# Splitting an expert's first weight matrix into two 16-bit halves: stepping reads exchanged for stepping writes

## The chip, the cores and the metric

The kernel runs on one core of one Trainium2 chip. The metric is the time on the device in microseconds (us), the median of several executions. The engines are named as the profile names them: PE (matrix multiply), PEld (its weight load), DVE (vector engine), ACT (scalar engine), POOL (GpSimd) and SP (which issues transfers).

## The reference

The program is an attention over channels, whose output feeds a mixture of eight experts, each token going to one of them:

```python
qn = q / (norm(q, axis=1) + 1e-6);  kn = k / (norm(k, axis=1) + 1e-6)
a = softmax(kn.transpose(0, 2, 1) @ qn / tau)          # 256 x 256 for each of 4 batches
x = (v @ a).reshape(20224, 256)
e_idx = argmax(x @ w_gate, axis=1)                     # one of 8 experts for each token
for e in range(8):
    h = maximum(x[mask_e] @ w1[e], 0)                  # w1[e]: 256 x 1024
    out[mask_e] = gate_w * sigmoid(x @ w_output_gate)[e] * (h @ w2[e])   # w2[e]: 1024 x 256
```

The inputs are float32.

## The kernel before, in words

**Stages.** The grams (`gram`, L372) build k'q for four batches from streams of q and k; this takes the first part of the span together with `mix` (L528), which multiplies v by the attention matrix, picks an expert for each token (`route`) and scatters the rows by expert into memory. Then `blocks` (L1019) takes units of 256 tokens (the last ones of 128): it fetches rows and weights of an expert, forms h (`h_part`, L958), and from the unit before it y (`y_part`, L983), and scatters the result. The blocks of the first experts begin while `mix` still runs.

**Two halves for every number.** PE works on 16-bit floats for the experts. Each number is split into hi, its 16-bit rounding after a scale by a power of two, and lo, the 16-bit rounding of what is left. A product takes three matmuls (hi hi, hi lo, lo hi): L972 to L974 for h, L996 to L998 for y.

**The split of the weights** is `split` (L317), called once for w1 (`half` 0) and once for w2 (`half` 1) of each of the eight experts, 16 times in all. A tile `raw` of 128 partitions x 2048 float32 holds the matrix as it lies in memory. L328 takes the sum of squares in two passes of 1024 columns (written into hi as scratch), L333 and L334 add over the partitions, `root2` makes the scale `wsw`. Then the loop at L348 walks over cuts: for each, ACT writes hi (L349) and DVE writes lo = raw * scale - hi (L350), reading raw and hi.

For w2 there are two cuts of 1024 columns, read and written in order. For w1 there are four of 512 elements, and the order of the columns changes: a partition holds two rows of w1 of 1024 columns, `(c m f)` with c of 2, m of 128, f of 8, and h_part wants them as `(c f m)`, so that 128 neighbouring columns of a weight load have the same f. Neighbouring m are 8 float32 apart in `raw` (32 bytes); neighbouring f are 128 16-bit floats apart in hi and lo (256 bytes).

**Where the splits stand in the order of work.** Each engine runs its instructions in the order in which they were written. The split of expert 0 (`prep_first`) writes straight into the buffer that PE reads (`wbuf`) and stands within `mix` of the last batch. The splits of experts 1 to 7 (`prep`) go into `whi` and `wlo` (one buffer each, used by w1 and w2 in turn) and are stored to memory by `keep` (L358, issued by SP) for the blocks to fetch; they are spread over the steps of `blocks`. A step of `blocks` is one h_part and one y_part, 12 matmuls each for a full unit, with ACT's L976 (hi of h) and DVE's L977 (lo of h) behind the h_part. The generator yields after each second cut, so that a split of w1 puts two L349 on ACT and two L350 on DVE into one step and two more of each into the next, each pair behind the step's L976 and L977. PE reads h one unit later, from the tile `hb`; h's sums stand in PSUM in one of four buffers (`ps_x`) until L976 and L977 have read them.

Of the kernel before, what the change touches and what calls it, by code (L numbers as in the profile page):

```python
# [20 lines left out]
P = 128  # L21
# [17 lines left out]
def tile_colnorm_attention_then_top1_moe(  # L39
# [23 lines left out]
    CC = C // P  # L63
    FC = FF // P
# [154 lines left out]
    @contextmanager  # L219
    def behind(*engines):  # L220
        with ExitStack() as held_back:
            for e in engines:
                if e in last:
                    held_back.enter_context(tc.issue_after(last[e]))
            yield
# [10 lines left out]
    def pause(n):  # L236
        for _ in range(n):
            yield
# [17 lines left out]
    def root2(ss, kk, scale, inv):  # L256

        e = sm.tile(list(ss.shape), I32, tag="r2e", name="r2e")
        nc.vector.tensor_scalar(
            out=e, in0=ss.bitcast(I32), scalar1=24, scalar2=23,  # L260
            op0=ALU.logical_shift_right, op1=ALU.logical_shift_left,
        )
        nc.vector.tensor_scalar(
            out=scale.bitcast(I32), in0=e, scalar1=-1.0, scalar2=float((189 + kk) << 23), op0=ALU.mult, op1=ALU.add
        )
        nc.vector.tensor_scalar(
            out=inv.bitcast(I32), in0=e, scalar1=float((65 - kk) << 23), scalar2=None, op0=ALU.add
        )
# [19 lines left out]
    def prep(first, end, tag):  # L288
        todo = []
        for r in range(first, end):  # L290
            for half in range(2):
                with behind("SP"):
                    raw = load_raw(r, half, tag)
                todo.append(lambda raw=raw, half=half, r=r: in_turn(split(raw, half, r), "ACT", "DVE", "PE"))
                yield
                if len(todo) > AHEADW:
                    yield from todo.pop(0)()
        for f in todo:
            yield from f()

    def prep_first():

        raws = []
        for half in range(2):
            raws.append(load_raw(0, half, "raw"))
            yield
        yield from pause(RWAIT)
        parts = [in_turn(split(raw, half, 0), "ACT", "DVE", "PE") for half, raw in enumerate(raws)]
        for i in range(6):
            for part, since in zip(parts, (0, 2)):  # L310
                if i >= since:
                    next(part, None)
            yield
        for part in parts:
            yield from part

    def split(raw, half, r):  # L317

        rows = slice(r * P, (r + 1) * P)
        if r == 0:  # L320
            hi, lo = (wbuf[half][:, 0, n * HW1 : (n + 1) * HW1] for n in range(2))
        else:
            hi = big.tile([P, HW1], F16, tag="sp", name=f"whi{r}_{half}", bufs=1)
            lo = big.tile([P, HW1], F16, tag="sl", name=f"wlo{r}_{half}", bufs=1)
        ss = sm.tile([P, 2], F32, tag="wss", name="wss")
        for i in range(2):
            a = slice(i * HW1 // 2, (i + 1) * HW1 // 2)
            nc.scalar.activation(hi[:, a], raw[:, a], AF.Square, accum_out=ss[:, i : i + 1])  # L328
            yield
        yield from pause(WAITW)  # L330
        w_ps = ps_x.tile([P, 512], F32, tag="x", name="w_ps")
        tot = sm.tile([P, 1], BF16, tag="wtot", name="wtot")
        nc.vector.tensor_tensor(out=tot, in0=ss[:, 0:1], in1=ss[:, 1:2], op=ALU.add)  # L333
        nc.tensor.matmul(w_ps[:, 0:1], onesb, tot, start=True, stop=True)  # L334
        sw = sm.tile([P, 1], F32, tag="wsw", name="wsw")
        root2(w_ps[:, 0:1], KW, sw, invw[:, half, r : r + 1])

        if half == 0:
            src, dh, dl = (
                raw.rearrange("p (c m f) -> p c f m", c=CC, f=FC),  # L340
                hi.rearrange("p (c f m) -> p c f m", c=CC, f=FC),
                lo.rearrange("p (c f m) -> p c f m", c=CC, f=FC),
            )
            cuts = [(slice(None), c, slice(i, i + FC // 2)) for c in range(CC) for i in (0, FC // 2)]
        else:
            src, dh, dl = raw, hi, lo
            cuts = [(slice(None), slice(i * HW1 // 2, (i + 1) * HW1 // 2)) for i in range(2)]
        for i, a in enumerate(cuts):  # L348
            nc.scalar.activation(dh[a], src[a], AF.Copy, scale=sw)  # L349
            nc.vector.scalar_tensor_tensor(  # L350
                out=dl[a], in0=src[a], scalar=sw, in1=dh[a], op0=ALU.mult, op1=ALU.subtract
            )
            if i % 2:
                yield
        def keep():
            with behind("SP"):
                for n, part in enumerate((hi, lo)):
                    nc.sync.dma_start(wsc[half][rows, n * HW1 : (n + 1) * HW1], part)  # L358

        if r == 0:  # L360
            held.append(keep)
        else:
            keep()
        if half == 1:
            iw = invw[:, :, r : r + 1]
            nc.vector.tensor_tensor(out=iw[:, 0, :], in0=iw[:, 0, :], in1=iw[:, 1, :], op=ALU.mult)
            prepped.append(r)
# [763 lines left out]
```

## Time and profile before

| what | before |
|---|---|
| median of 3 runs | 1279.93 us (1278.78 to 1285.42) |
| the profiled execution, its span | 1285.2 us, span 1283.4 us |
| PE busy | 1201.1 us, 94% of the span |
| DVE, ACT, POOL busy | 702.2 us, 620.3 us, 572.5 us |
| L349 on 512 elements (w1), L350 on 512 elements (w1) | 32 each, 1217 and 1142 ns in experts 1 to 7 |
| L349 on 1024 elements (w2), L350 on 1024 elements (w2) | 16 each, 1141 and 1284 ns in experts 1 to 7 |

The profile was taken on one execution, 5.3 us above the median of the runs. "Busy" of PE counts its pipelined matmuls. A group's row gives the line, the engine, the operation, the tiles it writes and reads, the shapes, the count, its busy time and the mean time of one, and then how long the engine had been idle just before and what ended that. In the chain of waits each piece is followed back from the end of the program to what released it.

### The profile page before, as it was taken

The numbers are of one execution on the slowest core, as the hardware profiler recorded it, in microseconds if no ns is written. First come the engines' busy times: TensorE is split into PE (matmuls) and PEld (weight loads), VectorE is DVE, ScalarE is ACT, GpSimd is POOL, SyncE is SP. The second block draws the span as 40 slices with busy tenths as digits, with TensorE's granted clock in tenths as the row PEclk, the third lists the DMA queues.
The fourth block names the chain that finished last, engine by engine and source line by source line (L and its number), as shares of the span: only waits on it lengthen the run. The fifth ranks groups of instructions, "written<-read, shape, count | busy, mean of one in ns | idle before, by whom it ended". The sixth has DMA issues, their size and how long they took to land.

```text
span 1283.4 us, 27742 instructions
## 1 busy us (share of the span) xinstructions
PE 1201.1 (94%) x10412; PEld 1075.3 (84%) x10412; DVE 702.2 (55%) x2123; ACT 620.3 (48%) x1233; POOL 572.5 (45%) x561
## 2 busy tenths in 40 slices
PE   8999999997766989999999999999999899999998
PEld 7898888896755878888888888888888789999997
DVE  6666647544646765546464566544444454555552
ACT  5666557445633555545364556433333333444442
POOL 0004654555466123445454455544445454444443
PEclk9999999897989999999999999999999999999999
DMA  8976776754547895556555554843333534346743
GB/s 294 333 239 219 251 251 222 241 161 156 184 157 197 219 251 142 143 142 142 142 143 142 142 142 110 234 107 77 68 72 100 161 66 88 78 77 165 202 108 133
DMA packets 174594, 208.54 MB, mean 162 GB/s; under 512 B 120904, under 2 KB 123982, under 8 KB 169464
## 3 DMA queue, kind: packets, MB, share of 16 engines
q1 hardware_dynamic: 130312, 126.84, 35.7%
q0 software_dynamic: 43312, 79.73, 21.4%
q8 instruction: 84, 1.38, 0.4%
q14 instruction: 54, 0.44, 0.1%
q10 hardware_dynamic: 832, 0.16, 0.1%
HBM read 275.55 MB, written 61.41 MB: 263 GB/s over the span
## 4 chain that ended last, share of the span: by engine, by line
PE 75%; issue 8%; DMA 5%; DVE 4%; ACT 3%; POOL 2%; another core or an unknown queue 2%; POOLq 0%; SPq 0%; ACTq 0%; DVEq 0%
PE h_ps L974 9%; PE s_ps L409 9%; PE h_ps L972 9%; PE h_ps L973 9%; PE y_ps L998 9%; PE y_ps L996 9%; PE y_ps L997 9%; PE x_ps L549 3%; PE vt_ps L519 3%; PE x_ps L551 3%; PE x_ps L550 3%; DMA qk<-in_k_dram 2%; POOL out_dram L1009 1%; DMA wbuf<-wsc,wi 1%
## 5 line engine op out<-in xcount | busy, mean ns | idle before, releaser
L977 DVE SCALAR_TENSOR_TENSOR hb<-h_ps,hb 128x512 f16<-128x512 f32 (+1 forms) x360 | 227.1, 634 | 368.5 <-ACT hb L976 282.4
L972 PE MATMUL h_ps<-xt,wbuf 128*128 128x256 f16 (+1 forms) x1440 | 367.7, 263 | 8.5 <-issue 3.9
L974 PE MATMUL h_ps<-xt,wbuf 128*128 128x256 f16 (+1 forms) x1440 | 367.8, 263 | 3.6 <-issue 3.6
L973 PE MATMUL h_ps<-xt,wbuf 128*128 128x256 f16 (+1 forms) x1440 | 367.8, 263 | 3.5 <-issue 3.4
L996 PE MATMUL y_ps<-wbuf,hb 128*128 128x256 f16 x1296 | 354.4, 274 | 4.7 <-issue 3.4
L998 PE MATMUL y_ps<-wbuf,hb 128*128 128x256 f16 x1296 | 354.3, 274 | 3.6 <-issue 2.5
L997 PE MATMUL y_ps<-wbuf,hb 128*128 128x256 f16 x1296 | 354.4, 273 | 1.8 <-issue 1.6
L976 ACT ACTIVATE hb<-h_ps 128x512 f16<-128x512 f32 (+1 forms) x360 | 194.3, 550 | 328.8 <-PE h_ps L974 211.9
L627 POOL DMA_INDIRECT xs_d<-st,r_si x160 | 171.3, 1071 | 227.2 <-DVE r_si L623 91.5
L865 POOL DMA_INDIRECT wbuf<-wsc,wi x166 | 175.4, 1056 | 217.0 <-PE h_ps L974 154.0
L1009 POOL DMA_INDIRECT out_dram<-yo,b_id x162 | 168.9, 1043 | 76.0 <-issue 42.8
L972 PEld LDWEIGHTS <-wbuf 128*128 128x128 f16 x1440 | 141.6, 98 | 23.4 <-issue 5.5
L409 PE MATMUL s_ps<-qk 128*128 128x256 f32 x640 | 152.5, 389 | 8.8 <-DMA qk<-in_k_dram 6.3
L973 PEld LDWEIGHTS <-wbuf 128*128 128x128 f16 x1440 | 141.5, 98 | 21.0 <-issue 7.0
L974 PEld LDWEIGHTS <-wbuf 128*128 128x128 f16 x1440 | 141.6, 98 | 18.3 <-issue 4.6
L996 PEld LDWEIGHTS <-hb 128*128 128x128 f16 x1296 | 127.2, 98 | 21.7 <-issue 6.3
L998 PEld LDWEIGHTS <-hb 128*128 128x128 f16 x1296 | 127.2, 98 | 21.6 <-issue 4.6
L409 PEld LDWEIGHTS s_ps<-qk 128*128 128x128 f32 x640 | 120.8, 195 | 23.9 <-DMA qk<-in_q_dram 6.3
L997 PEld LDWEIGHTS <-hb 128*128 128x128 f16 x1296 | 127.2, 98 | 16.3 <-issue 2.1
L881 POOL DMA_INDIRECT xg<-xs_d,gi x49 | 50.8, 1037 | 178.5 <-DVE xr L947 157.7
L549 PE MATMUL x_ps<-ah,vh 128*128 128x272 f32 x320 | 104.5, 327 | 20.7 <-DVE rco L624 8.2
L397 DVE TENSOR_TENSOR acc<-acc,sq 128x1024 f32<-128x1024 f32 x76 | 92.8, 1222 | 44.9 <-ACT sq L396 29.1
(196 smaller groups left out, 1497.2 us busy)
## 6 DMA issues: line engine op xcount, KB each, us to landing
qk<-in_q_dram SPq DMA_DIRECT2D x76, 256.0 KB
qk<-in_k_dram SPq DMA_DIRECT2D x76, 256.0 KB
v<-in_v_dram SPq DMA_DIRECT2D x32, 512.0 KB
raw<-in_moe_w_dram SPq DMA_DIRECT2D x16, 1024.0 KB
xg<-xs_d SPq DMA_DIRECT2D x30, 272.0 KB
wsc<-whi SPq DMA_DIRECT2D x14, 512.0 KB
wsc<-wlo SPq DMA_DIRECT2D x14, 512.0 KB
v<-in_v_dram SPq DMA_DIRECT2D x8, 480.0 KB
```

The lines of the kernel that those rows point to most:

```text
L409: nc.tensor.matmul(s_ps[:, c, :], kt[:, 1, t, c * P : (c + 1) * P], qt[:, 0, t, :], start=st == 0 and t0 == 0 and t == 0 and c == 0 and n ...
L627: ins = nc.gpsimd.indirect_dma_start(out=xs_d[:, :], out_offset=bass.IndirectOffsetOnAxis(ap=si[:np_, t : t + 1], axis=0), in_=st[:np_, t, ...
L865: nc.gpsimd.indirect_dma_start(out=wbuf[half][:, at_of(u), :], out_offset=None, in_=wsc[half][:end, :], in_offset=bass.IndirectOffsetOnAxi ...
L972: nc.tensor.matmul(hp, w1s[:, 0, c, fs], xh, start=fi == 0 and c == 0, stop=False, **KWM)
L973: nc.tensor.matmul(hp, w1s[:, 0, c, fs], xl, start=False, stop=False, **KWM)
L974: main(PE=nc.tensor.matmul(hp, w1s[:, 1, c, fs], xh, start=False, stop=fin, **KWM))
L976: main(ACT=nc.scalar.activation(hh, h_ps[:, :, :w], AF.Relu))
L977: ins = nc.vector.scalar_tensor_tensor(out=hb[:, 1, 2 * fp : 2 * fp + 2, :w], in0=h_ps[:, :, :w], scalar=0.0, in1=hh, op0=ALU.max, op1=ALU ...
L996: nc.tensor.matmul(y_ps[:, t, :], hb[:, 0, f, tsl], w2s[:, 0, f, :], start=st, stop=False, **KWM)
L997: nc.tensor.matmul(y_ps[:, t, :], hb[:, 0, f, tsl], w2s[:, 1, f, :], start=False, stop=False, **KWM)
L998: main(PE=nc.tensor.matmul(y_ps[:, t, :], hb[:, 1, f, tsl], w2s[:, 0, f, :], start=False, stop=fin, **KWM))
L1009: ins = nc.gpsimd.indirect_dma_start(out=out[:, :], out_offset=bass.IndirectOffsetOnAxis(ap=un["id"][:, t : t + 1], axis=0), in_=un["yo"][ ...
```

## The change

In the four cuts of w1, ACT and DVE now go through `raw` in the order in which it lies in memory, and write hi and lo in steps. Before, they went through hi and lo in order and read `raw` in steps. The cuts are now halves of m (64 x 8 elements) where they were halves of f (4 x 128); each is still 512 elements, and the place of every number in hi and lo is as it was.

```diff
         if half == 0:
             src, dh, dl = (
-                raw.rearrange("p (c m f) -> p c f m", c=CC, f=FC),
-                hi.rearrange("p (c f m) -> p c f m", c=CC, f=FC),
-                lo.rearrange("p (c f m) -> p c f m", c=CC, f=FC),
-            )
-            cuts = [(slice(None), c, slice(i, i + FC // 2)) for c in range(CC) for i in (0, FC // 2)]
+                raw.rearrange("p (c m f) -> p c m f", c=CC, f=FC),
+                hi.rearrange("p (c f m) -> p c m f", c=CC, f=FC),
+                lo.rearrange("p (c f m) -> p c m f", c=CC, f=FC),
+            )
+            cuts = [(slice(None), c, slice(i, i + P // 2)) for c in range(CC) for i in (0, P // 2)]
```

The instructions stand where they stood, on every engine; only the shape of L349 and L350 for w1 is another. Here is DVE at the split of w1 of expert 1, with what each instruction waits for (`wlo` is lo, `whi` is hi, `raw` the float32 weights, `hb` the h of a block):

```order
-L350 SCALAR_TENSOR_TENSOR wlo_0_5184<-raw_0_5076,wsw,whi_0_5183 128x512 [waits DMAHW6_49,Activation_49]
-L350 SCALAR_TENSOR_TENSOR wlo_0_5184<-raw_0_5076,wsw,whi_0_5183 128x512 [waits Activation_49]
-L977 SCALAR_TENSOR_TENSOR hb<-h_ps,hb 128x512 [waits Activation_49]
-L350 SCALAR_TENSOR_TENSOR wlo_0_5184<-raw_0_5076,wsw,whi_0_5183 128x512 [waits Activation_49] x2
+L350 SCALAR_TENSOR_TENSOR wlo_0_5184<-raw_0_5076,wsw,whi_0_5183 128x64x8 [waits DMAHW6_49,Activation_49]
+L350 SCALAR_TENSOR_TENSOR wlo_0_5184<-raw_0_5076,wsw,whi_0_5183 128x64x8 [waits Activation_49]
+L977 SCALAR_TENSOR_TENSOR hb<-h_ps,hb 128x512 [waits Activation_49]
+L350 SCALAR_TENSOR_TENSOR wlo_0_5184<-raw_0_5076,wsw,whi_0_5183 128x64x8 [waits Activation_49] x2
```

Nothing moved, and each L350 waits for the same engines as before. On ACT, at the same place (`whi` is written by L349):

```order
-L349 ACTIVATE whi_0_5183<-raw_0_5076,wsw 128x512 [waits DVE_49,Activation_49]
-L349 ACTIVATE whi_0_5183<-raw_0_5076,wsw 128x512
-L976 ACTIVATE hb<-h_ps 128x512 [waits PE_49]
-L349 ACTIVATE whi_0_5183<-raw_0_5076,wsw 128x512 [waits Activation_49]
-L349 ACTIVATE whi_0_5183<-raw_0_5076,wsw 128x512
+L349 ACTIVATE whi_0_5183<-raw_0_5076,wsw 128x64x8 [waits DVE_49,Activation_49]
+L349 ACTIVATE whi_0_5183<-raw_0_5076,wsw 128x64x8
+L976 ACTIVATE hb<-h_ps 128x512 [waits PE_49]
+L349 ACTIVATE whi_0_5183<-raw_0_5076,wsw 128x64x8 [waits Activation_49]
+L349 ACTIVATE whi_0_5183<-raw_0_5076,wsw 128x64x8
```

Here too the order and the engines waited for are the same: although the two cuts of one c now interleave in hi, the second L349 does not wait for DVE.

## The prediction, made before the changed kernel ran

> **What bounds the kernel now.** I read first the shares of the engines and the chain of waits, then the stretches in which splits run, then the rows of the two changed lines.
>
> ```profile
> PE 1201.1 (94%) x10412; PEld 1075.3 (84%) x10412; DVE 702.2 (55%) x2123; ACT 620.3 (48%) x1233; POOL 572.5 (45%) x561
> PE 75%; issue 8%; DMA 5%; DVE 4%; ACT 3%; POOL 2%; another core or an unknown queue 2%; POOLq 0%; SPq 0%; ACTq 0%; DVEq 0%
> ```
>
> PE is the bound, with 82 us of the span not busy. ACT and DVE are half idle; a change in them counts only where PE runs dry behind them. Where the splits run, the windows say (columns: stretch, length, busy time and count of PE, PEld, DVE, ACT, POOL, granted clock, transfers):
>
> ```profile
> 345.00:356.00 11.00, 8.85 (x66) 8.47 (x65) 9.70 (x26) 11.00 (x21) 9.15 (x7) 0.84 0.22 78
> 420.00:440.00 20.00, 19.80 (x183) 17.50 (x181) 15.44 (x57) 12.76 (x22) 4.47 (x5) 1.00 0.86 218
> 600.00:660.00 60.00, 59.23 (x540) 52.32 (x538) 33.62 (x93) 32.24 (x59) 30.70 (x29) 1.00 0.54 139
> 700.00:835.00 135.00, 15.92 (x14) 1.00 0.58 155
> L349 ACT ACTIVATE wbuf<-raw,wsw x6: 1187/1226/1302, 345.7 to 353.5; 128x512 f16<-128x512 f32 x4, 128x1024 f16<-128x1024 f32 x2
> L349 ACT ACTIVATE whi<-raw,wsw x42: 1132/1212/1232, 430.3 to 828.6; 128x512 f16<-128x512 f32 x28, 128x1024 f16<-128x1024 f32 x14
> ```
>
> (The fourth row counts L349 alone on ACT.) Two regimes. From 345 to 356 us, where expert 0 is split inside the last batch's mixing, ACT is busy for 11.00 of 11 us and PE for 8.85: **ACT bounds this stretch.** From 430 to 829 us, experts 1 to 7 are split and PE is full: 59.23 of 60 us, 0.110 us for each of 540 matmuls. Here the splits cost only what PE waits for behind them:
>
> ```profile
> PE w_ps L334 <- DVE wtot L333: 5.8, 6, 4.0
> PE y_ps L998 <- DVE hb L977: 1.2, 3, 0.6
> PE y_ps L998 <- DVE hb L977: 0.2, 1, 0.2
> PE y_ps L998 <- DVE hb L977: 0.6, 1, 0.6
> ```
>
> The first two rows are PE's waits from 320 to 860 us (total, times, longest), the last two those at the w1 splits of 430 and 738 us. So of seven w1 splits two just reach PE, by 0.2 and 0.6 us; five stay below it. The wait for `wtot` is for the squares ahead of the changed lines.
>
> **The change, part by part.** Nothing is added, moved or taken away: 4 of L349 and 4 of L350 for each of eight experts, 32 and 32, change their access patterns. Their price before, beside the same lines and their neighbours in order:
>
> ```profile
> L349 ACT ACTIVATE whi<-raw,wsw 128x512 f16<-128x512 f32 x28 | 32.7, 1217 | 7.3 <-DVE invw L266 7.3
> L349 ACT ACTIVATE whi<-raw,wsw 128x1024 f16<-128x1024 f32 x14 | 15.3, 1141 | 15.7 <-DVE invw L266 15.5
> L946 ACT ACTIVATE xr<-xg,b_sx 128x256 f16<-128x256 f32 x162 | 74.2, 500 | 81.3 <-DVE b_sx L249 76.8 <-DVE wtot L333 2.1 <-DVE p2e L248 1.7
> L350 DVE SCALAR_TENSOR_TENSOR wlo<-raw,wsw,whi 128x512 f16<-128x512 f32 x28 | 31.3, 1142 | 9.7 <-ACT whi L349 9.7
> L350 DVE SCALAR_TENSOR_TENSOR wlo<-raw,wsw,whi 128x1024 f16<-128x1024 f32 x14 | 17.4, 1284 | 8.5 <-ACT whi L349 7.3 <-issue 1.2
> L947 DVE SCALAR_TENSOR_TENSOR xr<-xg,b_sx,xr 128x256 f16<-128x256 f32 x162 | 71.9, 479 | 3.5 <-ACT xr L946 1.9 <-issue 0.8 <-ACT whi L328 0.7
> ```
>
> L946 and L947 do on 256 elements in order what L349 and L350 do. ACT in order: (1141 - 500) / 768 = 0.835 ns an element, so 500 + 256 x 0.835 = 714 ns for 512; with the 32-byte steps it takes 1217, **503 ns more** (0.98 an element). DVE in order: (1284 - 479) / 768 = 1.048 ns, so 747 ns for 512; it takes 1142, **395 ns more** (0.77 an element).
>
> *What ACT saves and pays.* The stepping read goes, a stepping write comes: one stream in order, one not, as before. No row shows a long stepping write; the nearest are short:
>
> ```profile
> L605 ACT CAST st<-ids 128x8 int32<-128x8 f32 x20 | 4.2, 212 | 3.4 <-DVE acc L421 1.9 <-DVE r_d L584 0.7 <-issue 0.6
> L601 ACT ACTIVATE r_og<-r_og 128x8 f32<-128x8 f32 x20 | 4.3, 214 | 10.2 <-DVE r_og L600 6.1 <-DVE r_os L598 3.7 <-issue 0.4
> ```
>
> L605 writes 8 words at steps of a row of `st` (272 words), L601 8 in order: no difference, where a price like the read's would be 8 ns, about their scatter; tens of ns an element are excluded. Ends: 714 ns (stepping writes are free) and 1720 (they cost twice what the reads did, 1217 + 503, since each is half a word). I take 1217, the read's price, because the nearest row of size is the same line with one stepping stream.
>
> *What DVE saves and pays.* Reading `raw` in steps goes. But L350 also reads hi, which now lies in steps for it, and it writes lo in steps: **one stepping stream becomes two.** The price of the second input can be read:
>
> ```profile
> L728 DVE SCALAR_TENSOR_TENSOR tb_sl<-jf,tb_res 128x62 f32<-128x62 f32 x1 | 0.2, 216 | 0.0
> L731 DVE SCALAR_TENSOR_TENSOR tb_sl<-tb_sl,tb_g 128x62 f32<-128x62 f32 x1 | 0.3, 265 | 0.0
> L738 DVE SCALAR_TENSOR_TENSOR tb_ex<-tb_res,tb_g 128x62 f32<-128x62 f32 x1 | 0.3, 257 | 0.0
> L490 DVE SCALAR_TENSOR_TENSOR al<-s_sb,se,ah 128x256 fp32r<-128x256 f32 x8 | 3.6, 482 | 0.7 <-ACT ah L489 0.7
> ```
>
> All three of the first are the same operation on 62 elements; L731 and L738 read the second input at steps of 9 words (36 bytes). They take 41 to 49 ns more, 0.66 to 0.79 an element, which is what L350 pays on its first input. (L490 reads at steps of 8 bytes and pays nothing against L947's 479: the step's size matters.) So the stepping read of hi alone brings 747 + 340 = 1087 to 747 + 405 = 1152 ns: DVE has nothing to win, even where its writes are free. Ends: 1087, and 1547 where the write adds another 395. I take 1200: the two streams step at the same elements, so I let them mostly overlap.
>
> The Trainium skill bears on this choice in "Vector Engine (DVE) Microarchitecture Reference", section "Measured stream behaviour on trn2": with one source hopping every element it has 1.73 ns an element, with the output hopping 1.71, with all three 1.98, and it says that read and write penalties only partly add. The before row agrees with the first, (1142 - 211) / 512 = 1.82 with 211 ns of fixed time. By its 1.98 an estimate for L350 is 211 + 512 x 1.98 = 1225 ns; by its row of 2.5 for the output stepping 24 words, 1491.
>
> *The sum.* In the first stretch ACT changes by 4 x 0 and DVE by 4 x (1.200 - 1.158) = 0.2 us, behind ACT's 11.00 of 11 us: 0 to 0.2 us. In the PE stretch look at two steps around 431 us, ACT's rows first:
>
> ```profile
> 430.31 2.33 ACT L349 ACTIVATE whi<-raw,wsw 128x512 f16<-128x512 f32 x2
> 432.55 0.58 ACT L976 ACTIVATE hb<-h_ps 128x512 f16<-128x512 f32 x1
> 433.03 2.33 ACT L349 ACTIVATE whi<-raw,wsw 128x512 f16<-128x512 f32 x2
> 431.56 2.25 DVE L350 SCALAR_TENSOR_TENSOR wlo<-raw,wsw,whi 128x512 f16<-128x512 f32 x2 [1.54 <-ACT whi L349]
> 433.73 0.68 DVE L977 SCALAR_TENSOR_TENSOR hb<-h_ps,hb 128x512 f16<-128x512 f32 x1
> 434.33 2.21 DVE L350 SCALAR_TENSOR_TENSOR wlo<-raw,wsw,whi 128x512 f16<-128x512 f32 x2
> L350 DVE SCALAR_TENSOR_TENSOR wbuf<-raw,wsw,wbuf 128x512 f16<-128x512 f32 x4 | 4.6, 1158 | 0.7 <-ACT wbuf L349 0.7
> ```
>
> A pair and its L976 take ACT 2.72 us, a pair and its L977 take DVE 2.77, against 24 x 0.110 = 2.63 us of PE for a step. They fall behind by 0.1 us a step, and PE lives on what was done before. Behind the pair stand L977 and the L913 to L947 of the next unit, and for L977 waits PE. Four L350 of 58 ns more make DVE 0.23 us later at each split; at the two splits without reserve PE waits 0.23 us longer each, 0.5 us. Sum: 0 + 0.2 + 0.5, **0.7 us at most, on 1285.2 us of the profiled execution**. That execution lay 5.3 us above the median; I put the sum on the median, 1279.93 + 0.6 = **1280.5 us**. If the cover were gone everywhere, the same 58 ns would cost 28 x 0.058 = 1.6 us.
>
> **The rivals.** *Stepping writes are free on ACT.* [...] ACT saves 4 x 0.503 = 2.0 us in its own stretch. In the PE stretch DVE's first L350 starts 0.5 us earlier, which can take away no more than the 0.2 + 0.6 us that PE waits: 2.8 us, 1277.1 us. The waits for `wtot` are the only other reserve near, 5.8 us; earlier splits might win part of it. Were all of it won, 8.6 us, 1271.3.
>
> *Stepping 16-bit writes cost more than the reads did: slower.* Place: DVE's L977 behind the L350 pairs, and PE's y behind it. Each half word goes to another place than the last, and L350 has it beside a stepping read. At the upper ends, L350 takes 405 ns more and L349 503. A split then comes 4 x 0.405 = 1.6 us later by DVE, 4 x 0.503 = 2.0 by ACT. With DVE alone: the two splits without reserve cost 3.2 us, the five others between 0 and 1.6 each, 4.0 in the middle, the first stretch 0.5: about 8 us. With ACT too: 2.0 in the first stretch, 4.0, and 5.0 from the five: 11 us, 1291. I put the rival at 1289. It decides from about 6.4 us on, when L350 reaches some 1.45 us. Against it: L605, and that each write goes to a port other than the read's.
>
> *The two interleaved cuts bring a wait that was not there* (the second L349 for DVE's first L350, about 1.1 us a pair). Against it stands the order of both engines, in which the waits are on the same engines. 2 in 100. *That the change does nothing at all*, because both patterns are run in one order, is excluded by the new shape of 64 x 8.
>
> The Trainium skill has a rule, "SBUF — State Buffer", under the 16-byte cachelines of section "Door 1: The DMA port swizzle", that an access to a new line each time is penalised, whichever way. L490's free 8-byte steps and L731's paid 36-byte ones agree for reads. By it both patterns pay, and it gives my forecast for ACT.
>
> **How the numbers follow.** A difference below 0.5%, 6.4 us, is about what a measurement of this kernel can tell from none: its three runs span 6.6 us. Forecast (nothing seen, within 3 us): 0.55, which gives 0.52 same, 0.02 slower, 0.01 faster. ACT's writes free: 0.23; of this 0.15 stays within 0.5%, 0.08 goes beyond. Slower rival: 0.20, of which 0.16 beyond 0.5% and 0.04 within. New wait: 0.02, slower. Sums: faster 0.09, same 0.71, slower 0.20. The range for 8 in 10 reaches from below the free writes, 1274, to about the slower rival, 1290.
>
> **What will show it.** L349 on 512 elements near 1217 ns (1100 to 1350) and L350 near 1200 (1090 to 1300) bear the two prices out; 714 on ACT is the first rival, 1450 or more on DVE the second. ACT should still fill its stretch near 345 us, with its four L349 at about 1.26 us; PE's waits for L977 at the w1 splits should stay below 2 us in total. The forecast is wrong if L350 is above 1450 ns and the total still within 3 us (then PE had more reserve than I give it), or if the prices hold and the time moves by more than 6 us (then something else than these two lines moved).

## The result and the profile after

| | kernel before | changed kernel |
|---|---|---|
| median, us (lowest to highest, runs) | 1282.06 (1278.78 to 1285.42, 4) | 1326.05 (1318.88 to 1332.19, 4) |
| profiled execution, us | 1285.2 | 1332.19 |
| its span, us | 1283.4 | 1330.5 |

The changed kernel is slower: the ratio is 1.0341 with a 95% interval of 1.0264 to 1.0418, 44 us by the medians. (Here and below, runs over 1.5% slower than the fastest of their kernel are left out of the ratios, so that a ratio is not always the quotient of the two medians.) The forecast was 1280.5 us, "nothing seen", with a range up to 1290 us. It was wrong.

Shares of the engines and the chain of waits, changed kernel:

```profile
PE 1223.3 (92%) x10412; PEld 1085.7 (82%) x10412; DVE 742.9 (56%) x2123; ACT 658.5 (49%) x1233; POOL 573.8 (43%) x561
PE 52%; issue 6%; DVE 5%; DMA 4%; ACT 2%; POOL 2%; another core or an unknown queue 1%; POOLq 0%; DVEq 0%; ACTq 0%; SPq 0%
```

The counts of instructions are those of before. ACT has 38 us more to do and DVE 41. PE is still the engine with the least idle time, and the chain, which ran through PE for 75% before, now does so for 52%.

The rows of the changed lines, changed kernel (form and count, then busy us and mean ns of one, then the idle time before):

```profile
L349 ACT ACTIVATE whi<-raw,wsw 128x512 f16<-128x512 f32 x28 | 67.9, 2673 | 6.8 <-DVE invw L266 6.4 <-issue 0.4
L350 DVE SCALAR_TENSOR_TENSOR wlo<-raw,wsw,whi 128x512 f16<-128x512 f32 x28 | 67.0, 2542 | 18.8 <-ACT whi L349 13.2 <-issue 5.5
L349 ACT ACTIVATE wbuf<-raw,wsw 128x512 f16<-128x512 f32 x4 | 9.8, 2716 | 0.0
L350 DVE SCALAR_TENSOR_TENSOR wlo<-raw,wsw,whi 128x1024 f16<-128x1024 f32 x14 | 17.4, 1281 | 8.7 <-ACT whi L349 6.2 <-issue 2.4
```

Here is the surprise. A stepping L349 takes 2673 ns, where reading in steps took 1217; L350 takes 2542 where it took 1142. The forecast had 1217 and 1200, and its upper ends were 1720 and 1547. The split of w2, which steps nowhere, is unchanged in the last row (1284 before). So each w1 split has 4 x 1.456 = 5.8 us more on ACT and 4 x 1.400 = 5.6 us more on DVE.

**Where the 47.1 us between the two spans lie.** I measured from the start of one w1 split (its first L349) to the start of the next. The windows below (columns: stretch, length, busy time and count of PE, PEld, DVE, ACT, POOL, granted clock, transfers) cover five such stretches together, the second to the sixth. Before:

```profile
471.80:795.10 323.30, 318.49 (x2890) 281.58 (x2888) 186.09 (x525) 170.99 (x310) 151.59 (x145) 1.00 0.56 140
```

Changed, the same work:

```profile
480.10:831.60 351.50, 329.37 (x2887) 284.90 (x2886) 210.81 (x525) 194.19 (x311) 155.15 (x145) 0.97 0.51 129
```

The work is the same (2890 and 2887 matmuls), but the five stretches together are 351.5 - 323.3 = 28.2 us longer, 5.6 us a split. Of this PE is idle for 22.1 us where it was for 4.8, so 17.3 us are waiting. The other 10.9 us are PE "busy" longer for the same matmuls at a granted clock of 0.97 where it was 1.00. The remaining 18.9 us of the difference are spread: 4.0 us ahead of the first of these seven splits (expert 0's stretch in the main), 4.3 and 6.5 us in the stretches after the first and the seventh split, 4.1 us in the long rest, where w1 is no longer split. Not all of these are waits for h: in the stretch after the seventh split PE waits 3.7 us for weights from memory, and in the rest one such wait is 6.3 us where it was 2.5.

The main waits of PE in those five stretches (total, times, longest), before and then changed:

```profile
PE w_ps L334 <- DVE wtot L333: 1.3, 4, 0.8
PE y_ps L998 <- DVE hb L977: 0.6, 1, 0.6
```

```profile
PE y_ps L998 <- DVE hb L977: 11.6, 8, 2.3
PE y_ps L996 <- DMA wbuf<-wsc,wi: 1.8, 1, 1.8
PE y_ps L996 <- ACT hb L976: 1.8, 2, 1.6
```

It is the wait that the slower rival named: PE's y matmuls behind L977 on DVE, and L977 behind the L350 pairs. L977 and L976 together account for 12.8 of the 17.3 us. The chain of waits through one split (start, duration, what) shows both parts of the loss:

```profile
548.21 2.58 ACT whi L349
...
550.81 4.79 DVE wlo L350 x2
555.61 0.53 DVE hb L977
...
556.18 0.28 PE y_ps L998
556.46 0.11 PE y_ps L996
...
556.99 0.21 PE h_ps L974
557.20 0.21 PE h_ps L972
...
559.98 0.21 PE y_ps L997
560.19 0.12 PE y_ps L998
560.31 0.11 PE y_ps L996
```

One L349 and two L350 keep L977 waiting from 548.21 to 555.61, 7.4 us, where before the same stretch of the chain ran from 430.31 to 433.73, 3.4 us. PE had stopped for 2.25 us when it came to L998 at 556.18. Then, from 556.8 to 560.1 us, matmuls follow each other every 0.21 us instead of every 0.11: about 16 matmuls at twice the time, some 1.6 us more.

That second part was no term of the forecast. In the timeline of PE the five stretches hold six such runs of 16 slow matmuls. Four of them follow a wait for L977, one a wait of 1.85 us for weights and one a stop of 2.12 us that the profile calls issue. In the two splits whose longest wait is 1.2 us (those at 618.6 and 689.3) none follows for some 10 us. The length of a stop alone does not decide it, though: a stop of 2.24 us at 442.23 was followed by matmuls at the full rate. The Trainium skill, "TensorE: Matmul & The Clock Gate", in "What's actually happening", describes a clock that falls to half after an idle window of about 3.4 us and rises again after as much busy time. The halved rate and the 3.4 us of its length agree with this trace; its length of the idle time does not, since here a stop of 2.25 us was enough. What decides it is left open.

### The profile page after: what moved, and what is told of

Its sections match the earlier page's. It is cut to its first block, busy times and chain, and to the rows that moved or that the text cites. A ratio compares the mean times of both kernels' runs of the same rounds, so it can differ in the third digit from the quotient of the medians.

```text
span 1330.5 us, 27742 instructions
## 1 busy us (share of the span) xinstructions
PE 1223.3 (92%) x10412; PEld 1085.7 (82%) x10412; DVE 742.9 (56%) x2123; ACT 658.5 (49%) x1233; POOL 573.8 (43%) x561
## 4 chain that ended last, share of the span: by engine, by line
PE 52%; issue 6%; DVE 5%; DMA 4%; ACT 2%; POOL 2%; another core or an unknown queue 1%; POOLq 0%; DVEq 0%; ACTq 0%; SPq 0%
PE y_ps L998 9%; PE y_ps L996 9%; PE y_ps L997 9%; PE h_ps L974 9%; PE h_ps L973 9%; PE h_ps L972 8%; DMA wbuf<-wsc,wi 3%; DVE wlo L350 2%; ACT whi L349 1%; DMA wsc<-whi 1%; POOL out_dram L1009 1%; DVE hb L977 1%; POOL wbuf L865 1%; ACT hb L976 0%
## 5 line engine op out<-in xcount | busy, mean ns | idle before, releaser
L977 DVE SCALAR_TENSOR_TENSOR hb<-h_ps,hb 128x512 f16<-128x512 f32 (+1 forms) x360 | 229.6, 642 | 366.9 <-ACT hb L976 290.5
L972 PE MATMUL h_ps<-xt,wbuf 128*128 128x256 f16 (+1 forms) x1440 | 371.7, 266 | 17.7 <-DMA wbuf<-wsc,wi 9.3
L974 PE MATMUL h_ps<-xt,wbuf 128*128 128x256 f16 (+1 forms) x1440 | 372.5, 266 | 3.7 <-issue 3.6
L973 PE MATMUL h_ps<-xt,wbuf 128*128 128x256 f16 (+1 forms) x1440 | 372.3, 266 | 3.6 <-issue 3.3
L998 PE MATMUL y_ps<-wbuf,hb 128*128 128x256 f16 x1296 | 357.5, 276 | 17.1 <-DVE hb L977 16.0
L976 ACT ACTIVATE hb<-h_ps 128x512 f16<-128x512 f32 (+1 forms) x360 | 198.5, 562 | 329.5 <-PE h_ps L974 251.1
L865 POOL DMA_INDIRECT wbuf<-wsc,wi x166 | 173.9, 1048 | 228.1 <-PE h_ps L974 155.2
L972 PEld LDWEIGHTS <-wbuf 128*128 128x128 f16 x1440 | 142.9, 99 | 32.5 <-DMA wbuf<-wsc,wi 10.5
L409 PE MATMUL s_ps<-qk 128*128 128x256 f32 x640 | 155.2, 394 | 9.5 <-DMA qk<-in_k_dram 6.3
L973 PEld LDWEIGHTS <-wbuf 128*128 128x128 f16 x1440 | 143.0, 99 | 23.8 <-issue 8.6
L974 PEld LDWEIGHTS <-wbuf 128*128 128x128 f16 x1440 | 143.1, 99 | 21.6 <-issue 6.6
L998 PEld LDWEIGHTS <-hb 128*128 128x128 f16 x1296 | 128.3, 99 | 36.1 <-DVE hb L977 19.1
```

The source lines that it names most:

```text
L409: nc.tensor.matmul(s_ps[:, c, :], kt[:, 1, t, c * P : (c + 1) * P], qt[:, 0, t, :], start=st == 0 and t0 == 0 and t == 0 and c == 0 and n ...
L865: nc.gpsimd.indirect_dma_start(out=wbuf[half][:, at_of(u), :], out_offset=None, in_=wsc[half][:end, :], in_offset=bass.IndirectOffsetOnAxi ...
L972: nc.tensor.matmul(hp, w1s[:, 0, c, fs], xh, start=fi == 0 and c == 0, stop=False, **KWM)
L973: nc.tensor.matmul(hp, w1s[:, 0, c, fs], xl, start=False, stop=False, **KWM)
L974: main(PE=nc.tensor.matmul(hp, w1s[:, 1, c, fs], xh, start=False, stop=fin, **KWM))
L976: main(ACT=nc.scalar.activation(hh, h_ps[:, :, :w], AF.Relu))
```

## The experiments

Each run is compared with the kernel before on its own chip, since chips differ by more than the effect. Before took 1286.03 us beside the two one-engine runs and the spread run; 1220.69 beside the control of the spread run, the first doubled run, expert 0 alone and the first version without steps; and 1299.62 beside the others.

Two questions were open. Is the price one of the written pattern, or of two engines that write into the same region at the same time? And does the time come from that price where DVE and ACT stand before PE, or from something else that the change moved?

### The price of each pattern by itself

512 elements, six times each, engines apart, and at the end both at once. The patterns that decide (`hop(t, s)` has neighbours s elements apart and returns to the next column after eight; `walk(t, s)` moves on by s and never returns; `runs` and `rung` write r neighbours before each hop):

```python
nc.scalar.activation(**act(mf(H), mf(raw)))               # L67  all in order
nc.scalar.activation(**act(in4(H), step8(raw)))           # L69  read in steps (before)
nc.scalar.activation(**act(hop(H, 128), mf(raw)))         # L71  write in steps (changed)
nc.scalar.activation(**act(walk(H, 16), mf(raw)))         # L77  one half word in each 32 bytes
nc.scalar.activation(**act(walk(H, 2), mf(raw)))          # L79  one half word in each 4 bytes
nc.scalar.activation(**act(runs(H, 2), runs_src(raw, 2))) # L81  pairs of half words, 256 bytes apart
nc.scalar.activation(**act(hop(F, 64), mf(raw)))          # L85  32-bit words, 256 bytes apart
nc.vector.scalar_tensor_tensor(**dve(mf(L), mf(raw), mf(H)))              # L95  all in order
nc.vector.scalar_tensor_tensor(**dve(hop(L, 128), mf(raw), hop(H, 128)))  # L99  changed
nc.vector.scalar_tensor_tensor(**dve(mf(L), mf(raw), hop(H, 128)))        # L101 only hi read in steps
nc.vector.scalar_tensor_tensor(**dve(hop(L, 128), mf(raw), mf(H)))        # L103 only lo written in steps
nc.vector.scalar_tensor_tensor(**dve(rung(L, 2), mr(raw, 2), mr(H, 2)))   # L111 pairs of half words, 32 bytes apart
nc.vector.scalar_tensor_tensor(**dve(hop(G, 64), mf(raw), mf(H)))         # L115 32-bit words, 256 bytes apart
```

> Leaves out the whole computation: on 512 elements in 128 partitions, ACT's scaled copy and DVE's raw * scale - hi run six times each in a number of access patterns, first ACT, then DVE, and at the end both at once in the changed pattern. In the changed kernel L349 took 2673 ns and L350 2542, which is 4.66 and 4.55 ns an element on the fixed times. Theory W (a stepping 16-bit write has its own price on each engine): ACT alone in the changed pattern 2.6 to 2.7 us; DVE with only the output stepping 2.5, with only hi read in steps 1.1, with both 2.5; both engines at once no more than alone. Theory C (the price comes of both engines stepping at once): each alone 1.2 to 1.3 us, and 2.6 at once. What the price hangs on, if W: if half words (a write of part of a word), then 32-bit writes in the same steps cost 1.2 us or less, a half word alone in its word at any step 2.6, and runs of two half words 1.2; if the step of 256 bytes, then steps of 264 bytes cost 1.2 and 32-bit writes at 256 bytes 2.6; if coming back to the neighbouring half word soon after, then a walk that never comes back costs 1.2 and the steps of 264 bytes 2.6.

Groups by line, the run of patterns:

```profile
L71 ACT ACTIVATE H<-raw,sw 128x512 f16<-128x512 f32 x6 | 15.4, 2568 | 0.2
L103 DVE SCALAR_TENSOR_TENSOR L<-raw,sw,H 128x512 f16<-128x512 f32 x6 | 15.0, 2492 | 0.2
L99 DVE SCALAR_TENSOR_TENSOR L<-raw,sw,H 128x512 f16<-128x512 f32 x6 | 14.9, 2484 | 0.0
L77 ACT ACTIVATE H<-raw,sw 128x512 f16<-128x512 f32 x6 | 14.4, 2393 | 0.0
L85 ACT ACTIVATE F<-raw,sw 128x512 f32<-128x512 f32 x6 | 8.1, 1342 | 0.0
L69 ACT ACTIVATE H<-raw,sw 128x512 f16<-128x512 f32 x6 | 7.3, 1215 | 0.2
L115 DVE SCALAR_TENSOR_TENSOR G<-raw,sw,H 128x512 f32<-128x512 f32 x6 | 6.5, 1084 | 0.0
L101 DVE SCALAR_TENSOR_TENSOR L<-raw,sw,H 128x512 f16<-128x512 f32 x6 | 6.5, 1084 | 0.2
L79 ACT ACTIVATE H<-raw,sw 128x512 f16<-128x512 f32 x6 | 5.0, 832 | 0.1
L81 ACT ACTIVATE H<-raw,sw 128x512 f16<-128x512 f32 x6 | 5.0, 830 | 0.2
L111 DVE SCALAR_TENSOR_TENSOR L<-raw,sw,H 128x512 f16<-128x512 f32 x6 | 4.5, 752 | 0.2
L95 DVE SCALAR_TENSOR_TENSOR L<-raw,sw,H 128x512 f16<-128x512 f32 x6 | 4.4, 736 | 90.8 <-ACT H L92 90.8
L67 ACT ACTIVATE H<-raw,sw 128x512 f16<-128x512 f32 x6 | 4.3, 721 | 0.2
```

What follows, from the rows:

- The price is there with one engine alone: 2568 ns on ACT (changed kernel 2673), 2484 on DVE (2542). With both at once it rises by 5%, to 2691 and 2626 ns. Contention between the two is not the cause.
- It is the write. Only lo written in steps takes DVE 2492 ns; with hi read in steps too 2484. The stepping read, 1084 ns alone, is hidden under the write altogether.
- It is the *single half word, far from the one written before it*. Steps without any return (L77) cost about the same as the changed pattern, so it isn't that the same region is gone over eight times. Nor is it the 256 bytes: steps of 264 bytes took 2478 ns on ACT and 2414 on DVE. 32-bit words at the same 256 bytes cost 1342 and 1084. Pairs of half words cost 830 and 752, close to in order, and so do single ones 4 bytes apart (832 on ACT, 790 on DVE). So "at any step", as the expectation had it, is wrong; where between 4 and 32 bytes the price begins was not measured. Above in order, a lone half word costs (2568 - 721) / 512 = 3.6 ns on ACT and (2492 - 736) / 512 = 3.4 ns on DVE, a lone 32-bit word 1.2 and 0.7. Runs of four half words took 752 ns on DVE but 1197 on ACT; ACT's test read its source in steps of 32 bytes, and L69's stepping read alone takes 1215, so that row says nothing on the write.

Why a half word whose neighbour isn't written with it costs so much (that the rest of its word has to be fetched first, say) is not shown by these rows, and the cheap single ones 4 bytes apart speak against that simple form. The Trainium skill, "Vector Engine (DVE) Microarchitecture Reference", "Measured stream behaviour on trn2", gives 1.71 ns a word where the output hops each time, for 32-bit words. L115 agrees, (1084 - 211) / 512 = 1.71; the half words, at (2492 - 211) / 512 = 4.46, lie outside what it states.

### One engine's half of the change at a time

The two lines get their patterns and cuts apart; ACT walks the changed way and DVE the old, or the reverse. In both, each pair of L349 is written ahead of its pair of L350, and the planner (which lays out the order of the instructions on the engines ahead of the run) moved a few in the mix. No run makes this rewriting alone, so what it costs by itself is not known.

```diff
+            of_act, of_dve = views("new"), views("old")    # the second run: "old", "new"
...
+        for n in range(0, len(of_act), 2):
+            for s, dh, dl in of_act[n : n + 2]:
+                nc.scalar.activation(dh, s, AF.Copy, scale=sw)
+            for s, dh, dl in of_dve[n : n + 2]:
+                nc.vector.scalar_tensor_tensor(
+                    out=dl, in0=s, scalar=sw, in1=dh, op0=ALU.mult, op1=ALU.subtract
+                )
+            yield
```

> Only ACT's hi of w1 is written in steps, DVE's lo is made as before (hi read in order, lo written in order). Theory W: L349 2.67 us, L350 1.14; four L349 add 5.8 us to a split on ACT, DVE waits for them, and PE for DVE: 1283 + 5.8 in the first stretch + 7 x (3 to 5.8) = 1310 to 1330 us. Theory C: L349 1.2 to 1.7 us and 1280 to 1290 us.

> Only DVE goes over w1 in the new way: hi read in steps, lo written in steps; ACT writes hi in order and reads raw in steps as before. Theory W: L350 2.54 us, L349 1.22; DVE is 5.6 us later at each split, less in the first stretch, where ACT sets the pace: 1283 + 4 + 7 x (2.5 to 5.6) = 1305 to 1326 us. Theory C: L350 1.2 to 1.7 us and 1280 to 1290 us. If e1 and e2 both lose nearly all of the 44 us, the two prices overlap in time and one alone is enough.

ACT's half alone: 1314.65 us, ratio 1.0187 (1.0103 to 1.0272). DVE's half alone: 1312.75 us, ratio 1.0221 (1.0148 to 1.0294). L990 and L991 are L976 and L977 here. Groups of ACT's half alone, then PE's waits in it from 430 to 900 us:

```profile
L363 ACT ACTIVATE whi<-raw,wsw 128x512 f16<-128x512 f32 x28 | 67.9, 2672 | 6.2 <-DVE wsw L263 6.2
L365 DVE SCALAR_TENSOR_TENSOR wlo<-raw,wsw,whi 128x512 f16<-128x512 f32 x28 | 30.8, 1142 | 48.0 <-ACT whi L363 33.2 <-issue 14.8
```

```profile
PE y_ps L1012 <- DVE hb L991: 9.8, 10, 2.1
PE y_ps L1010 <- ACT hb L990: 5.7, 4, 4.1
```

The same two views of DVE's half alone:

```profile
L365 DVE SCALAR_TENSOR_TENSOR wlo<-raw,wsw,whi 128x512 f16<-128x512 f32 x28 | 67.0, 2593 | 16.8 <-ACT whi L363 12.0 <-issue 4.8
L363 ACT ACTIVATE whi<-raw,wsw 128x512 f16<-128x512 f32 x28 | 32.9, 1225 | 7.6 <-DVE wsw L263 7.6
```

```profile
PE y_ps L1012 <- DVE hb L991: 17.9, 15, 3.3
PE y_ps L1010 <- ACT hb L990: 2.1, 3, 1.8
```

The prices stay with the lines. Each engine alone already makes PE wait and loses more than half of what both lose. By the middle values the two halves sum to 4.1% where the whole is 3.4%, as it would be if the two engines' delays partly run side by side. The intervals don't exclude that they simply add. Both times lie in the ranges expected from a price of each engine's own.

### The same price, spread out

The changed pattern, but the w1 of experts 1 to 7 in eight cuts of 256 elements, one cut each per step of the planner, whose rates are raised so that the splits still end in time. The control does the same to the kernel before.

```diff
-    SOON, SRATE = 20, 0.9
-    WRATE = 0.45
+    SOON, SRATE = 20, 1.39
+    WRATE = 0.695
...
+            fine = 1 if r == 0 else 2
+            w = P // (2 * fine)
+            cuts = [(slice(None), c, slice(i, i + w)) for c in range(CC) for i in range(0, P, w)]
...
-            if i % 2:
+            if i % 2 or len(cuts) == 8:
```

> The changed kernel, with w1 of experts 1 to 7 split in eight cuts of 256 elements, each in a step of its own, and the rate at which splits are advanced raised so that they end when they did. Theory E (the price shows because a pair of cuts with its L976 or L977 no longer fits into PE's step of 2.63 us): one cut takes 286 + 256 x 4.66 = 1.48 us on ACT and 1.38 on DVE, with 0.6 to 0.7 us for h a step of 2.1 us, which fits; PE's waits for L977 go from 16 to a few us and the time to 1288 to 1300 us, though ACT and DVE are as busy as in the changed kernel. Rival (what ACT and DVE spend is lost in any order, or PE and the transfers are slowed by the stepping writes themselves): 1315 to 1330 us.

> The kernel before, its w1 of experts 1 to 7 split in eight cuts of 256 elements and advanced at the raised rate, as in the spread version of the changed kernel (1299.9 us): the control for the spreading itself. If the spreading costs nothing: 1280 to 1288 us, and of the 44 us some 15 stay when spread. If it costs something of its own (later squares, more instructions): 1288 to 1296, and the spread changed kernel is then within 5 to 10 us of its control, which is the first stretch.

Spread, changed pattern: 1299.89 us, ratio 1.0107 (1.0046 to 1.0168). Spread, old pattern, on the next chip: 1222.54 us, ratio 1.0055 (1.0016 to 1.0094). Three views of the spread run with the changed pattern: the shares, ACT's group, and three of PE's waits from 400 to 900 us.

```profile
PE 1208.5 (93%) x10412; PEld 1076.6 (83%) x10412; DVE 744.9 (57%) x2151; ACT 661.1 (51%) x1261; POOL 574.4 (44%) x561
```

```profile
L351 ACT ACTIVATE whi<-raw,wsw 128x256 f16<-128x256 f32 x56 | 78.9, 1436 | 8.6 <-DVE invw L266 8.6
```

```profile
PE w_ps L334 <- DVE wtot L333: 10.6, 6, 3.5
PE y_ps L998 <- ACT hb L978: 4.5, 2, 3.5
PE y_ps L1000 <- DVE hb L979: 1.0, 3, 0.4
```

ACT and DVE have as much to do as in the changed kernel (661.1 and 744.9 us; 658.5 and 742.9 there), yet PE waits 1.0 us for L977 (L979 here) where the five stretches of the changed kernel alone had 11.6, and about two thirds of the loss are gone. (Of the 4.5 us for L976, L978 here, 3.5 are one wait at 444 us, behind L328.) Half of what stays also shows in the control, where spreading alone costs 0.5%, with PE waiting 12.1 us for `wtot`. So it isn't the added 80 us of work on two half-idle engines that costs; it is that they stand in one piece of two cuts between two L977.

### The price without the pattern

Every L349 and L350 of w1 issued twice in the old patterns: 84% of ACT's added time (4 x 1.217 of 5.8 us), no stepping write.

```diff
+            again = 2 if half == 0 else 1
+            for _ in range(again):
+                nc.scalar.activation(dh[a], src[a], AF.Copy, scale=sw)
+            for _ in range(again):
+                nc.vector.scalar_tensor_tensor(
...
```

> The kernel before, with each L349 and each L350 of w1 issued twice over, so that a cut takes 2 x 1.217 = 2.43 us on ACT and 2 x 1.142 = 2.28 on DVE with no stepping write anywhere (in the changed kernel 2.67 and 2.54). Theory T (only the time on ACT and DVE at these places counts): it adds 83% and 81% of what the change added, so about 0.82 x 44 = 36 us over the kernel before, 1312 to 1325 us. Rival (the stepping writes do harm beside their own time, to PE's loads, POOL's descriptors or transfers): less than 20 us over the kernel before.

> Each L349 and L350 of w1 issued twice, no stepping write, beside the changed kernel on one chip. Theory T (only the time on ACT and DVE counts): 0.82 of the changed kernel's loss. Rival (the stepping writes harm others too): half of it or less. The first try gave 1.016 +- 0.008 on a faster chip.

It took 1235.28 us, ratio 1.0159 (1.0082 to 1.0236), and on the last chip 1311.78 us, ratio 1.0181 (1.0061 to 1.0301), beside 1.0314 (1.0200 to 1.0427) for the changed kernel there. That is slower, and about half of the loss instead of the four fifths expected: by the expectation's own prices nearer to its rival, that the stepping writes harm others too. The changed kernel's trace speaks against that rival where PE does not wait. From 619 to 632 us, while L349 and L350 write in steps, PE does 122 matmuls in 13.00 us, and so it does before the change from 602 to 615 us; POOL's L865 takes 1048 ns where it took 1056. The timeline of ACT in one split of the second doubled run (start, duration) says why the run is no clean test:

```profile
539.97 2.34 ACT L351 ACTIVATE whi<-raw,wsw 128x512 f16<-128x512 f32 x2 [0.47 <-DVE invw L266]
542.22 0.57 ACT L979 ACTIVATE hb<-h_ps 128x512 f16<-128x512 f32 x1
542.69 2.33 ACT L351 ACTIVATE whi<-raw,wsw 128x512 f16<-128x512 f32 x2
544.93 0.58 ACT L979 ACTIVATE hb<-h_ps 128x512 f16<-128x512 f32 x1
```

Here an L979 (the L976 of before) comes after each 2.3 us of splitting. This is the best of the seven splits: in the others the pieces without an L979 last from 1.2 to 4.6 us, and three of the seven splits have one of 4.6. In the changed kernel all fourteen pieces last 4.8 to 4.9 us, since its two instructions of twice the length were left in the old places. PE waits 7.2 us for L980 (L977) from 430 to 900 us, where it waits 15.7 us in the same way in the changed kernel. This agrees with the spread run, and leaves the exact share of the pattern's price that a planned placement hides unmeasured.

### Expert 0 alone, and experts 1 to 7 alone

```diff
-        if half == 0:
+        if half == 0 and r == 0:      # the complement: r > 0
...
```

> Only the split of w1 of expert 0 is made in the changed way; experts 1 to 7 as before. The share of the first stretch: ACT fills it and takes 4 x 1.46 = 5.8 us more there, so 5 to 6 us over the kernel before, 1286 to 1291 us, if nothing behind it takes up the slack; the other 38 us are then those of the seven splits beside the blocks, 5.5 each. If it costs 0 to 2 us, the stretch had cover and the seven splits cost over 6 us each; if over 10, the delay grows behind the stretch.

> The changed kernel on the chip of the next three runs, since the chips differ (the kernel before took 1280 us on two of them and 1220 on a third). Ratio 1.030 to 1.042 as before if the loss is of the engines' own time; L349 2.67 us and L350 2.54 in any case.

> The complement of the run with expert 0 alone: w1 of experts 1 to 7 split in the changed way, expert 0's as before. If the two parts add up: the changed kernel's time less 6 to 14 us. From PE's waits for L977 and L976 and the lower clock behind them: 25 to 38 us over the kernel before.

| | median, us | before on that chip | ratio (95%) |
|---|---|---|---|
| expert 0 alone | 1231.37 | 1220.69 | 1.0121 (1.0045 to 1.0196) |
| changed kernel again | 1324.55 | 1299.62 | 1.0314 (1.0200 to 1.0427) |
| experts 1 to 7 alone | 1326.17 | 1299.62 | 1.0288 (1.0191 to 1.0385) |

Without expert 0 nearly all of the loss is there: the later splits, in PE's full stretch, make it. How much expert 0 costs is not settled. By the difference of the last two rows it is 0.3%, with an uncertainty larger than that, and the two traces of before and changed lie 4.0 us apart after it; alone it cost 1.2%, about 15 us by the ratio, where 5 to 6 were expected. In that run's profile PE waits for something else:

```profile
PE w_ps L334 <- DVE wtot L333: 16.9, 4, 11.2
```

The longest of these waits goes back to ACT's L328 at 425.18 us, which stood 13.58 us for the store of the previous hi. In the changed kernel the same wait is 1.0 us in all, and 5.8 before. That the delay of expert 0 meets a later transfer there would explain it; I did not test what decides it.

### No stepping at all

If the order of the hidden columns is free, neither side has to step. Let column f of block m stay where the raw weights have it, and let w2 be loaded so that its rows come in the same order: partition p then holds the rows f * 128 + p, in pieces of 1 KB. The w1 split runs in order, in four cuts of 512.

```diff
-    wraw = (w1.rearrange("e (p c) f -> (e p) (c f)", c=CC), w2.rearrange("e (p f) d -> (e p) (f d)", f=FC))
+    wraw = (w1.rearrange("e (p c) f -> (e p) (c f)", c=CC), w2.rearrange("e (f p) d -> p (e f) d", f=FC))
...
+            nc.sync.dma_start(raw.rearrange("p (f d) -> p f d", f=FC), wraw[1][:, bass.ds(row, FC), :])
...
+        src, dh, dl = raw, hi, lo
+        k = 4 if half == 0 else 2
+        cuts = [(slice(None), slice(i * HW1 // k, (i + 1) * HW1 // k)) for i in range(k)]
```

> No stepping at all: hidden column f * 128 + m stands for (f, m), so that w1 is split in the order in which it lies, in four cuts of 512, and w2 is loaded so that partition p holds its rows f * 128 + p (eight pieces of 1 KB for each partition where it was one of 8 KB). L349 0.72 us and L350 0.74 on 512 elements. ACT saves 4 x 0.5 = 2.0 us in the first stretch and DVE's 0.2 and 0.6 us of PE's waits go: 2 to 4 us under the kernel before, a ratio of 0.997 to 0.999; with w2's transfers slower by their smaller pieces it could be no gain.

It took 1207.38 us (12 runs) against 1220.69, ratio 0.9935 (0.9904 to 0.9966): on that chip a little faster than the kernel before, by about 8 us where 2 to 4 were expected. Where the rest of the gain comes from was not followed up. Groups of it:

```profile
L347 DVE SCALAR_TENSOR_TENSOR wlo<-raw,wsw,whi 128x512 f16<-128x512 f32 x28 | 19.9, 748 | 5.8 <-ACT whi L346 5.8
L346 ACT ACTIVATE whi<-raw,wsw 128x512 f16<-128x512 f32 x28 | 18.6, 713 | 4.8 <-DVE invw L267 4.8
```

These are the two prices that the prediction worked out for in order, 714 and 747. A further variant sent the squares of L328 to a tile of their own, so that they need not wait for the store of hi:

```diff
+        junk = one.tile([P, HW1 // 2], F16, tag="sqj", name="sqj")
...
-            nc.scalar.activation(hi[:, a], raw[:, a], AF.Square, accum_out=ss[:, i : i + 1])
+            nc.scalar.activation(junk, raw[:, a], AF.Square, accum_out=ss[:, i : i + 1])
```

> The version without any stepping (0.9935 of the kernel before), and the squares of L328 written to a scratch tile of their own in place of hi, so that they no longer wait until the last hi has been stored. PE's waits for the sum of the squares (7.1 us in the version without stepping) should fall to 2 us or less; L349 then waits for the store itself, later. 2 to 5 us under the version without stepping: 0.990 to 0.993; if the wait only moves to L349 and holds up L976 behind it, no gain.

1282.39 us against 1299.62, ratio 0.9952 (0.9900 to 1.0004). PE's waits for `wtot` went from 7.1 to 4.0 us, not to the 2 us or less that were expected, and no gain beyond the first version shows. On this chip the interval does not exclude that nothing was won against the kernel before.

## Why the prediction was wrong, step by step

- **What bounds the kernel** was read rightly. PE is full from 430 to 829 us, two of the splits just reached it, and the loss came at exactly this place, in PE's waits for L977.
- **"I take 1217, the read's price"** is the step that failed. L349 writing in steps takes 2673 ns, above the upper end of 1720 as well. That end put twice the read's 503 ns on the 714 in order, "since each is half a word"; measured, it is 2673 - 714 = 1959 ns, 3.9 times the read's. The evidence taken for writes, L605, writes eight 32-bit words, and 32-bit words are indeed cheap (1342 ns for 512). It is no evidence on half words, and neither row that was quoted had any. The Trainium skill's rule of cachelines, in "SBUF — State Buffer", does not tell reads from writes and names no price; that it gave the forecast for ACT, the same price both ways, was the prediction's reading, and it fails: L71 and L69 differ by more than 1.3 us.
- **"I take 1200"** for L350 failed for the same reason: 2542 ns measured, upper end 1547. Its parts held. The stepping read of hi alone takes 1084 ns (1087 to 1152 were read out of the trace), and the two streams do overlap, fully: 2484 with both, 2492 with the write alone. But what they overlap under is 2.5 us long.
- **The sum of 0.7 us** therefore had a term of 0.058 us for L350 where 1.40 belongs, and 0 for L349 where 1.46 belongs. It also let only "the two splits without reserve" reach PE. With 5.6 us a split, all seven do.
- **In the first stretch** "0 to 0.2 us" failed with ACT's zero. There ACT has 4 x 1.46 = 5.8 us more, and the next split begins 4.0 us later than before.
- **The rival that ended slower** had the mechanism and the place: half words, L977 behind L350, PE's y behind it, and the point from which it decides, 1.45 us. Its price was too small, 1289 us. Two things were missing besides the size. DVE waits for ACT's first L349, so a split moves by that 1.35 us too: from the first L349 to the end of the last L350 it took 6.2 us at 430.31 and 13.2 at 548.21, 7.0 more, where it counted four L350 or four L349. And it had no term for the lower rate of matmuls after PE has stopped, 10.9 us in the five stretches measured.
- **Free writes** and **a wait between the interleaved cuts** did not happen. The order of the instructions was unchanged, as said; that also meant that the doubled work stood where the shorter had stood.
- **The sign of the slower rival**, 1450 ns or more on DVE, is what the profile shows. The range of 1274 to 1290 was bounded by ends that came from reads. An operation with no row of its size in the trace deserved a range up to several times the nearest row, and a larger chance than 0.20 for the slower side.

About 19 of the 47.1 us between the two profiled executions lie outside the five stretches that were accounted for, and the 4.1 us of them in the long rest are within what two executions of one kernel differ by (1318.88 to 1332.19 us for this one). Within the five, some 4.5 of the 17.3 us of waiting are for weights and for what the profile calls issue; what brought them is not shown.

## What to carry to other kernels

When a change of layout must make one side step, let the read step, or write full words or pairs of half words; single half words in steps cost here more than twice a stepping read of the same length. Better, ask whether the order of an inner index is free: choosing it so that neither side steps was worth about 0.65% here, on one chip. And work added to a half-idle engine costs little in itself: what counts is the longest piece that stands between two instructions for which the full engine waits, so a price that the planner does not know must be put into its cuts by hand.

## What the runs showed of the hardware that was not expected

- A half word written far from the one before it costs 3.2 to 3.6 ns more an element than in order on both engines, whether 32 or 256 bytes lie between two of them (2393 and 2568 ns on ACT, 2364 and 2492 on DVE). A half word in every 4 bytes (832 and 790 ns) or pairs (830 and 752 ns) cost little more than in order (721 and 736).
- Reading half words in steps of 256 bytes is as cheap as reading 32-bit words in steps: 1084 ns on DVE, beside 1107 for the old pattern.
- Of eleven stops of PE of 1.5 to 3.0 us between 430 and 880 us, nine were followed within 1 us by about 3.4 us in which matmuls came every 0.21 us instead of every 0.11; those of 2.24 us at 442.23 and 1.63 us at 485.43 were not, and in the control of the spread run two stops of 2.28 us were not either. Where it came, a wait of 2.25 us cost some 1.6 us more than its own length.
